# Message passing on a graph, edges sorted on the core: sums of the sort on ScalarE, portions cut anew

## The chip, the cores and the metric

One core of a Trainium2 chip runs the kernel. Its engines are named as in the profile: PE (TensorE, matrix products), DVE (VectorE), ACT (ScalarE), POOL (GpSimd) and SP (SyncE, which here only issues DMAs). Each has one queue that is worked off in order; an instruction that waits holds up all behind it. The metric is the device time of one execution in microseconds. The kernel before takes 10198.05 us, the median of three runs from 10188.47 to 10201.76.

## What is computed

12500 nodes with 64 features, 800000 edges with 4 features each, and a two-layer network on each edge whose results are added up at the edge's target node:

```python
def reference(x, e_attr, src, dst, w1, b1, w2, b2):
    N, D = x.shape
    h_src = x[src]
    h_dst = x[dst]
    m_in = jnp.concatenate([h_src, h_dst, e_attr], axis=-1)
    h = _silu(m_in @ w1 + b1)
    msg = h @ w2 + b2
    return _segment_sum(msg, dst, N)
```

N = 12500, D = 64, H = 128, E = 800000; `src` and `dst` are drawn at random and come in no order.

## The kernel before

**Algebra.** The first layer is split: `x @ w1[:64]` is a table in HBM (`Atab`, one row of 128 floats per node, gathered by `src`), `x @ w1[64:128] + b1` is a table in SBUF (`Btab`, for the targets), and the edge's own features are multiplied on the fly. The second layer comes after the sum over edges, so that the loop over edges only adds up `silu(...)` and a count in `S`.

**Sorting.** The targets are cut into R = 98 buckets of 128 nodes. For the loop over edges each batch of 512 slots must hold edges of few buckets. So the kernel sorts the edges itself, in portions: the edges stand as 6250 columns of 128, a group is PT = 40 columns, and `_PORTIONS` says how many groups each portion has. For a portion, `rank` works out each edge's slot within its group, then where the group's rows go; `place` builds the rows (16 records of 16 bf16 values, `CS` = 16) by products with one-hot matrices on PE and POOL scatters them into `buf` in HBM (two DMAs per half group, line 870).

**The batch loop** (`run`, line 1093 on) goes over 1590 batches of 512 slots. For batch n it loads records six and more batches ahead (`load`, by SP), makes indices (`sources`), gathers four times 128 rows of `Atab` on POOL (`gather`, line 1042, six batches ahead, `NGA` = 7 buffers), turns the records (`copies`, `turn`: ACT `rp`, PE, ACT `pts`), codes them (`code`: PE, ACT `oT`), adds the terms (`pre` on PE, `join` on DVE), applies `silu` on ACT, makes the segment matrix (`onehot`: PE, ACT `sg`), multiplies (`seg`, PE) and adds to `S` (`accum`, DVE). `turn`, `code`, `pre` and `onehot` share two PSUM buffers named `px`.

**How the two run together.** Portion 0 is sorted alone, at the start (`sort(ports[0])`), with one step of the generator `tables` after each `TEVERY`-th yield of the sort: 26 steps that multiply and store `Atab`, then 14 that scale `Btab` (ACT and POOL). Then `run` starts. `sure[k]` is the number of batches that are filled for certain when portions 0 to k are placed (`expected_batches`, from mean and spread of random buckets); phase k is the batches up to `sure[k]`. During phase k the function `filler` pulls steps out of two generators, `place` of portion k+1 and `rank` of portion k+2 (in phase 0 first `rank` of portion 1 alone), at rates in proportion to `place_cost` and `rank_cost`, so that they end twelve batches before the phase does. What is left then is run off with no batches beside it. In the last phase nothing is left to sort.

**Order.** Work that the sort gives to PE or ACT isn't put into the queue at once but at four fixed places of a batch: `later_pe` before `onehot` (place 2, first half of the batch) or at the batch's end (place 3); `later_act`, which the kernel before has but does not call, at the batch's end for the first half, and after `code` of the next batch (place 1) for the second. In the start, with no batches (`clock["now"]` is None), everything is issued at once.

**`rank` in ticks.** A portion is ranked in banks of QS = 5 columns, eight to a group. One pass of the loop `while done < ng` is a tick: it builds the one-hot matrices of one bank (`buckets`, line 420, DVE), then does one of three things: `counts` of a group, `bases` of a group, or `slots` of a bank. `slots` has PE add up in PSUM (`xp`, from two buffers named `rx`) each edge's rank for all 98 buckets, and two ticks later DVE multiplies each of the bank's five columns with its one-hot matrix and adds up along the row (line 525, with `accum_out`), which picks the edge's own slot. Each tick ends with `yield HALF`: this lane then has to wait for the next half of a batch, so at most two ticks fit in a batch. `yield HOP` has it wait for the next batch; the steps after the ticks (lines 580 to 727) have some ten.

Of the kernel before, what the change touches and what calls it, by code (L numbers as in the profile page):

```python
# [10 lines left out]
F32 = mybir.dt.float32  # L11
# [4 lines left out]
AF = mybir.ActivationFunctionType  # L16
OP = mybir.AluOpType
ET = mybir.EngineType

EP = 128  # L20
GT = 20
GE = EP * GT
PT = 2 * GT
# [9 lines left out]
HALF = -2.0  # L33
SUB = 5
QS = 5
NOH = 13
NGA = 7
TEVERY = 8
TAIL = 32
FR = 256 // CS  # L40
BIG = 262144.0
# [34 lines left out]
def tile_mpnn(ctx, tc, x, e_attr, src, dst, w1, b1, w2, b2, out, portions):  # L76
    nc = tc.nc
# [5 lines left out]
    R = (N + 127) // 128  # L83
    NP = R * 128
    VE, SC, GP, PE = nc.vector, nc.scalar, nc.gpsimd, nc.tensor

    last = len(portions) - 1
# [81 lines left out]
    for i in range(2):  # L169
        VE.tensor_scalar(t40[:, i * GT:(i + 1) * GT], iop[:, 0:1].to_broadcast([128, GT]), 2.0 * PT + i, None,  # L170
                         op0=OP.is_equal)
# [62 lines left out]
    wk = ctx.enter_context(tc.tile_pool(name="wk", bufs=2))  # L234
# [130 lines left out]
    def later_pe(f):  # L365
        later(f, 0, 2 + clock["half"])
# [8 lines left out]
    def rank(p):  # L375
        k, ng, cols = p["k"], p["ng"], p["cols"]
# [4 lines left out]
        slT = wk.tile([128, CM], F32, name="slT")  # L381
# [13 lines left out]
        def codes(c0):  # L395

            cn = min(4 * PT, cols - c0)
            raw = raws.pop(c0)
            VE.tensor_copy(d16[:EP, c0:c0 + cn], raw[:EP, :cn, 0])
            hl = wk.tile([128, 4 * PT], U16, name="hl", bufs=1)  # L400
            VE.tensor_scalar(hl[:EP, :cn], d16[:EP, c0:c0 + cn], 7, None, op0=OP.logical_shift_right)
            bk = wk.tile([128, 4 * PT], BF, name="bk")
            VE.tensor_copy(bk[:EP, :cn], hl[:EP, :cn])
            bks[c0 // (4 * PT)] = bk
            fetch(c0 + 8 * PT)

        ohs, bT, soon = {}, {}, {}
        tick = dict(t=0, cost=0.0, out=0)
        ready = {}

        def dve(d, f, cost, end=False):

            soon.setdefault((tick["t"] + d, end), []).append((f, cost))

        def buckets(g, c):

            n = min(QS, gts[g] - c * QS)
            oh = wk.tile([128, QS, R], BF, name="ohb", bufs=NOH)
            s0 = g % 4 * PT + c * QS
            VE.tensor_tensor(oh[:EP, :n], iob[:EP].unsqueeze(1).to_broadcast([EP, n, R]),  # L420
                             bks[g // 4][:EP, s0:s0 + n].unsqueeze(2).to_broadcast([EP, n, R]), op=OP.is_equal)
            ohs[g, c] = oh
# [53 lines left out]
        def bases(g):  # L476


            box = {}

            def f():
                bp = ps.tile([128, 512], F32, name="rx", bufs=2)
                PE.matmul(bp[:NR, :R], exz[:R], idf[:R, :R], start=True, stop=False)
                PE.matmul(bp[:NR, :R], fz[:R], trw[:R, :R], start=False, stop=True)
                box["bp"] = bp
            later_pe(f)

            def d0():
                bi = wk.tile([128, 128], I32, name="bi", bufs=1)
                VE.tensor_copy(bi[:NR, :R], box["bp"][:NR, :R])  # L490
                box["bi"] = bi

            def d1():
                bi = box["bi"]
                VE.tensor_tensor(bi[:NR, :R], bi[:NR, :R], bits[:NR].to_broadcast([NR, R]), op=OP.bitwise_and)

            def d2():
                b = wk.tile([128, 128], BF, name="bT")
                VE.tensor_copy(b[:NR, :R], box["bi"][:NR, :R])
                bT[g] = b  # L500
            dve(2, d0, 200.0)
            dve(2, d1, 200.0, True)
            dve(3, d2, 150.0)

        def slots(g, c):

            box = {}
            n = min(QS, gts[g] - c * QS)

            def f():  # L510
                xp = ps.tile([128, 512], F32, name="rx", bufs=2)
                oh = ohs[g, c]
                PE.matmul(xp[:EP, :n * R], triB[:EP, :EP], oh[:EP, :n].rearrange("p s b -> p (s b)"),
                          start=True, stop=False)
                for i in range(n):
                    s_ = c * QS + i
                    PE.matmul(xp[:EP, i * R:(i + 1) * R], selB[:NR, s_:s_ + 1].to_broadcast([NR, EP]),  # L517
                              bT[g][:NR, :R], start=False, stop=i == n - 1)
                box["xp"] = xp
            later_pe(f)  # L520

            def one(i):
                s_ = g * PT + c * QS + i
                oh = ohs[g, c]
                VE.scalar_tensor_tensor(oh[:EP, i], box["xp"][:EP, i * R:(i + 1) * R], 0.0, oh[:EP, i],  # L525
                                        op0=OP.add, op1=OP.mult, accum_out=slT[:EP, s_:s_ + 1])

            def last():
                ohs.pop((g, c))
                tick["out"] -= 1  # L530
            for i in range(n):
                dve(2, lambda i=i: one(i), 171.0)
            dve(2, last, 0.0)

        fetch(0)
        fetch(4 * PT)
# [4 lines left out]
        while done < ng:  # L541
            t = tick["t"]
            for f, c in soon.pop((t, False), []):
                f()
                yield c
            if coded * 4 < ng and nq > (ends[4 * coded - 5] if coded > 1 else -1):
                codes(coded * 4 * PT)
                coded += 1
                yield 450
            if nq < len(banks) and tick["out"] < NOH - 1:  # L550
                buckets(*banks[nq])
                if nq in ends:
                    ready["q", banks[nq][0]] = t
                nq += 1
                tick["out"] += 1
                yield 580.0
            for f, c in soon.pop((t, True), []):
                f()
                yield c
            if counted < ng and ready.get(("q", counted), t + 1) <= t:  # L560
                counts(counted)
                ready["c", counted] = t + 3
                counted += 1
            elif based < counted and ready["c", based] <= t:
                bases(based)
                ready["b", based] = t + 3
                based += 1
            elif nx < len(banks) and ready.get(("b", banks[nx][0]), t + 1) <= t:
                slots(*banks[nx])
                if nx in ends:  # L570
                    ready["s", banks[nx][0]] = t + 2
                nx += 1
            while done < ng and ready.get(("s", done), t + 1) <= t:
                done += 1
            tick["t"] += 1
            next(zeros, None)
            yield HALF
        for _ in zeros:
            pass
        for t in sorted(soon):  # L580
# [2 lines left out]
        ng = -(-cols // GT)  # L583
# [344 lines left out]
    def sort(p):  # L928
        yield from rank(p)
        yield from place(p)  # L930

    def rank_cost(p):
        return p["ng"] * (PT / QS * (880 + 580) + 2300 + 450 / 4 + 1300) + 10000

    def place_cost(p):
        return p["ng"] * (2000 + 2300 + 460 + PT / SUB * 1900)
# [24 lines left out]
    for i in range(NPT):  # L961
        t = cst.tile([65, 512], BF, name=f"pts{i}")
# [3 lines left out]
    for i in range(3):  # L966
        t = cst.tile([128, 4, H + 1], F32, name=f"h{i}")
# [96 lines left out]
    sums = {}  # L1064
# [84 lines left out]
    for i, _ in enumerate(sort(ports[0])):  # L1149
        if i % TEVERY == 0:  # L1150
            next(tg, None)
# [21 lines left out]
    def filler(m, part):  # L1173
        if part == 0:
            k = phase[m]
            if m == 0 or phase[m - 1] != k:
                if work["lanes"]:
                    settle()
                    while work["lanes"]:
                        for lane in work["lanes"]:  # L1180
                            for _ in lane["gen"]:
                                pass
                        work["lanes"] = []
                        if work["todo"]:
                            begin(m)
                    clock["now"] = m - LL
                work["until"] = sure[k] - LL - 2
                jobs = []
                if k + 1 < len(ports):
                    p = ports[k + 1]  # L1190
                    if k == 0:
                        work["todo"].append([(rank_cost(p), lambda p=p: rank(p))])
                    jobs.append((place_cost(p), lambda p=p: place(p)))
                if k + 2 < len(ports):
                    p = ports[k + 2]
                    jobs.append((rank_cost(p), lambda p=p: rank(p)))
                if jobs:
                    work["todo"].append(jobs)
                    begin(m - LL)
            return  # L1200
# [45 lines left out]
    for b0 in range(0, R, 4):  # L1246
# [6 lines left out]
        op = ps.tile([128, 512], F32, name="so", bufs=2)  # L1253
# [3 lines left out]
        for i in range(bn):  # L1257
            VE.scalar_tensor_tensor(ot[:, i], b2c, S[:, b0 + i, H:H + 1], op[:, i * D:(i + 1) * D],  # L1258
                                    op0=OP.mult, op1=OP.add)
# [6 lines left out]

_INS = ['x', 'e_attr', 'src', 'dst', 'w1', 'b1', 'w2', 'b2']
_OUTS = [((12500, 64), 'float32')]
_PORTIONS = [12, 8, 7, 9, 9, 12, 13, 11, 12, 13, 13, 13, 13, 12]


# [23 lines left out]
```

## Time and profile before

| | |
|---|---|
| median of three runs | 10198.05 us |
| profiled execution | 10154.93 us |
| its span, first to last instruction | 10153.1 us |
| mean granted clock of PE | 0.897 of full |
| instructions | 256393 |
| DMA | 563.40 MB, mean 55 GB/s |

How to read it: "busy" is the time in which an engine works on instructions, "idle before" is its idle time just before the instructions of a group, with what ended it. Register, branch and semaphore instructions and the issuing of DMAs are not busy time. A window's row gives for each engine the busy time and in brackets the number of instructions, then PE's granted clock, the share of the DMA engines and GB/s. Releasers are inferred. The durations of POOL's instructions are rough.

In forty equal slices of the span, a digit being tenths of the slice, the engines go like this:

```profile
PE   7788898999898998888998988989988988887774
DVE  6977887988798887777988888878878875542221
ACT  2044354444444444544444444444444444445552
POOL 3477577777777777777777777777777777777772
PEclk7888898999999999998999998999999999887776
```

### The profile page before, as it was taken

The numbers are of one execution on the slowest core, as the hardware profiler recorded it, in microseconds if no ns is written. First come the engines' busy times: TensorE is split into PE (matmuls) and PEld (weight loads), VectorE is DVE, ScalarE is ACT, GpSimd is POOL, SyncE is SP. The second block draws the span as 40 slices with busy tenths as digits, with TensorE's granted clock in tenths as the row PEclk, the third lists the DMA queues.
The fourth block names the chain that finished last, engine by engine and source line by source line (L and its number), as shares of the span: only waits on it lengthen the run. The fifth ranks groups of instructions, "written<-read, shape, count | busy, mean of one in ns | idle before, by whom it ended". The sixth has DMA issues, their size and how long they took to land. (4 is left out here: it accounts for less than half of the span.)

```text
span 10153.1 us, 256393 instructions
## 1 busy us (share of the span) xinstructions
PE 8728.9 (86%) x83393; PEld 7245.2 (71%) x83574; DVE 7601.7 (75%) x34618; ACT 4492.5 (44%) x8743; POOL 7351.0 (72%) x7072
## 2 busy tenths in 40 slices
PE   7788898999898998888998988989988988887774
PEld 5566776777777777776777777777777776666663
DVE  6977887988798887777988888878878875542221
ACT  2044354444444444544444444444444444445552
POOL 3477577777777777777777777777777777777772
PEclk7888898999999999998999998999999999887776
DMA  2022222222222222222222223222222222222332
GB/s 56 8 56 61 49 53 64 47 65 53 67 48 49 66 53 69 55 54 70 51 52 69 54 51 70 54 57 66 55 52 68 54 52 58 55 53 57 57 57 36
DMA packets 1176600, 563.40 MB, mean 55 GB/s; under 512 B 990738, under 2 KB 1066061, under 8 KB 1175136
## 3 DMA queue, kind: packets, MB, share of 16 engines
q0 software_dynamic: 223584, 443.00, 17.6%
q1 hardware_dynamic: 948234, 99.40, 6.8%
q8 instruction: 752, 12.32, 0.5%
q14 instruction: 712, 5.83, 0.2%
q10 hardware_dynamic: 3318, 2.85, 0.1%
HBM read 471.78 MB, written 88.20 MB: 55 GB/s over the span
## 5 line engine op out<-in xcount | busy, mean ns | idle before, releaser
L1042 POOL DMA_INDIRECT ga<-Atab,ix x6360 | 6475.6, 1018 | 2109.0 <-issue 1532.5
L1024 ACT ACTIVATE oT<-px,inv 128x512 bf16<-128x512 f32 x1590 | 1092.9, 687 | 3355.2 <-PE px L1022 3343.6
L1075 PE MATMUL so<-h,sg 128*128 128x129 f32 x12720 | 2405.6, 316 | 135.8 <-DVE S L1082 111.4
L909 PE MATMUL pl<-mk,oh 128*128 128x256 bf16 x18750 | 2364.2, 282 | 41.0 <-DVE oh L861 21.8
L909 PEld LDWEIGHTS <-oh 128*128 128x128 bf16 x18750 | 1861.2, 101 | 383.6 <-DVE oh L861 50.7
L1075 PEld LDWEIGHTS so<-h,sg 128*128 128x128 f32 x12720 | 1837.7, 208 | 321.3 <-DVE S L1082 165.3
L861 DVE TENSOR_SCALAR oh<-io,lo 128x384 bf16<-128x384 bf16 x6250 | 1811.9, 325 | 0.0
L1082 DVE TENSOR_TENSOR S<-S,so 128x129 f32 x3180 | 902.0, 284 | 1089.8 <-PE so L1075 1020.5
L1049 DVE TENSOR_TENSOR ga<-px,ga 128x512 f32<-128x512 f32 x1590 | 1089.7, 685 | 756.0 <-DMA ga<-Atab,ix 446.0
L1035 PE MATMUL px<-Btab,oT 128*128 x12720 | 1608.5, 236 | 3.2
L1033 PE MATMUL px<-WE,pts 65*128 65x128 bf16 x6360 | 1387.7, 238 | 17.1 <-DVE ga L1049 15.7
L1018 ACT ACTIVATE pts<-px 64x512 bf16<-64x512 f32 x1590 | 932.9, 587 | 809.7 <-PE px L1016 787.8
L1058 ACT ACTIVATE sg<-px 128x512 f32<-128x512 f32 x1590 | 947.1, 596 | 771.9 <-PE px L1056 748.2
L525 DVE SCALAR_TENSOR_TENSOR ohb<-rx,ohb 128x98 bf16<-128x98 f32 x6250 | 1271.6, 251 | 16.3 <-PE rx L517 15.8
L1056 PE MATMUL px<-CT,pts 65*128 65x128 bf16 x6360 | 636.9, 224 | 720.3 <-DVE ga L1049 375.7
L1056 PEld LDWEIGHTS <-pts 65*128 65x128 bf16 x6360 | 490.3, 100 | 1055.8 <-issue 1013.5
L1035 PEld LDWEIGHTS <-oT 128*128 128x128 bf16 x12720 | 1157.5, 108 | 89.5 <-issue 22.3
L854 DVE TENSOR_TENSOR mk<-q,pay 128x640 int32<-128x640 int32 x1250 | 1026.2, 821 | 179.8 <-PE pl L909 176.0
L870 POOL DMA_INDIRECT buf<-cb,idx x626 | 777.8, 1243 | 363.0 <-ACT carry L883 148.0
L1062 ACT ACTIVATE h<-ga 128x512 f32<-128x512 f32 x1590 | 985.5, 620 | 0.0
L420 DVE TENSOR_TENSOR ohb<-iob,bk 128x490 bf16<-128x490 bf16 x1250 | 834.8, 668 | 0.1
L1016 PE MATMUL px<-idb,rp 128*64 128x128 bf16 x6360 | 695.2, 236 | 57.7 <-DVE ga L1049 27.9
(313 smaller groups left out, 9076.2 us busy)
## 6 DMA issues: line engine op xcount, KB each, us to landing
ga<-Atab,ix POOLq DMA_INDIRECT x6360
buf<-zero SPq DMA_DIRECT2D x257, 128.0 KB
pld<-buf SPq DMA_DIRECT2D x1590, 16.0 KB
el<-in_e_attr_dram SPq DMA_DIRECT2D x73, 160.0 KB
buf<-cb,idx POOLq DMA_INDIRECT x626
Atab<-ga SPq DMA_DIRECT2D x24, 256.0 KB
sr<-in_src_dram SPq DMA_DIRECT2D x73, 80.0 KB
raw<-in_dst_dram SPq DMA_DIRECT2D x35, 160.0 KB
```

The lines of the kernel that those rows point to most:

```text
L525: VE.scalar_tensor_tensor(oh[:EP, i], box["xp"][:EP, i * R:(i + 1) * R], 0.0, oh[:EP, i], op0=OP.add, op1=OP.mult, accum_out=slT[:EP, s_:s ...
L854: VE.tensor_tensor(mk[:EP, :sn], q[:EP, s0:s0 + sn].unsqueeze(3).to_broadcast([EP, sn, CS, 8]), pay[:EP, go + s0:go + s0 + sn].bitcast(I32 ...
L861: VE.tensor_scalar(oh[:EP, i], io3[:EP], lo[:EP, go + s0 + i:go + s0 + i + 1], None, op0=OP.is_equal)
L909: PE.matmul(pa[:, u, :] if u < 2 else pb[:, :CS * PC], oh_[:, u * 128:(u + 1) * 128], mv, **fl)
L1024: SC.activation(oT, oq, AF.Relu, scale=inv[:, 0:1])
L1033: PE.matmul(pr[:, sl], pts[n % NPT][:, sl], WE, start=True, stop=False)
L1035: PE.matmul(pr[:, sl], s["oT"][:, sl], Btab[:, ds(v[t // 2], 1), u, :], start=False, stop=u == 1)
L1042: GP.indirect_dma_start(out=ga[:, t, :], out_offset=None, in_=Atab, in_offset=bass.IndirectOffsetOnAxis(ap=s["ix"][:, t:t + 1], axis=0))
L1049: VE.tensor_tensor(g, s["pr"], g, op=OP.add)
L1056: PE.matmul(sq[:, sl], pts[n % NPT][:, sl], CT, start=True, stop=True)
L1062: SC.activation(hs[n % 3][:, :, :H], st[n]["ga"], AF.Silu)
L1075: PE.matmul(so[u], s["sg"][:, t * 128:(t + 1) * 128], hs[n % 3][:, t, :], start=t == 2 * u, stop=t > 2 * u)
```

## The change

Five edits.

1. The sums over a bank's columns move. DVE makes one product over the whole bank of five columns (490 elements a partition) from `xp` in PSUM and the one-hot matrices into a new float tile `pr` with four buffers; ACT then adds up each of its five rows of 98 with a Copy that has `accum_out`, in place, put into ACT's queue by `later_act`. The one-hot buffers and the PSUM tile are given back after the product. In `rank` a bank is one entry on the list of DVE work (cost 580) instead of six (five of 171 and one of 0), so one yield instead of six.
2. For the portions before `FAST` = 6, `yield HALF` comes only after each second tick, otherwise `yield 0.0`: up to four ticks fit in a batch.
3. `TEVERY` is 16 instead of 8: a step of `tables` after each sixteenth yield of the sort of portion 0.
4. `_PORTIONS` has 16 entries instead of 14, the first with 10 groups instead of 12; `rank_cost` counts 580 + 580 per bank instead of 880 + 580.
5. `dynamic_dma_scratch_size` is 4096 instead of 8192.

```diff
-TEVERY = 8
+FAST = 6
+TEVERY = 16
...
-            def one(i):
-                s_ = g * PT + c * QS + i
-                oh = ohs[g, c]
-                VE.scalar_tensor_tensor(oh[:EP, i], box["xp"][:EP, i * R:(i + 1) * R], 0.0, oh[:EP, i],
-                                        op0=OP.add, op1=OP.mult, accum_out=slT[:EP, s_:s_ + 1])
-
-            def last():
-                ohs.pop((g, c))
+            def d():
+                pr = wk.tile([128, QS * R], F32, name="pr", bufs=4)
+                VE.tensor_tensor(pr[:EP, :n * R], box["xp"][:EP, :n * R],
+                                 ohs.pop((g, c))[:EP, :n].rearrange("p s b -> p (s b)"), op=OP.mult)
                 tick["out"] -= 1
-            for i in range(n):
-                dve(2, lambda i=i: one(i), 171.0)
-            dve(2, last, 0.0)
+
+                def sums():
+                    for i in range(n):
+                        s_, row = g * PT + c * QS + i, pr[:EP, i * R:(i + 1) * R]
+                        SC.activation(row, row, AF.Copy, accum_out=slT[:EP, s_:s_ + 1])
+                later_act(sums)
+            dve(2, d, 580.0)
...
-            yield HALF
+            yield HALF if k >= FAST or tick["t"] % 2 == 0 else 0.0
...
-        return p["ng"] * (PT / QS * (880 + 580) + 2300 + 450 / 4 + 1300) + 10000
+        return p["ng"] * (PT / QS * (580 + 580) + 2300 + 450 / 4 + 1300) + 10000
...
-_PORTIONS = [12, 8, 7, 9, 9, 12, 13, 11, 12, 13, 13, 13, 13, 12]
+_PORTIONS = [10, 5, 7, 5, 8, 8, 12, 12, 12, 12, 12, 12, 10, 10, 11, 11]
...
-    nc = _bacc.Bacc("TRN2", target_bir_lowering=False, num_devices=1, dynamic_dma_scratch_size=8192)
+    nc = _bacc.Bacc("TRN2", target_bir_lowering=False, num_devices=1, dynamic_dma_scratch_size=4096)
```

## Prediction

> **What bounds the kernel now.** The page first: no engine of it is full by its busy share.
>
> ```profile
> span 10153.1 us, 256393 instructions
> PE 8728.9 (86%) x83393; PEld 7245.2 (71%) x83574; DVE 7601.7 (75%) x34618; ACT 4492.5 (44%) x8743; POOL 7351.0 (72%) x7072
> L1042 POOL DMA_INDIRECT ga<-Atab,ix x6360 | 6475.6, 1018 | 2109.0 <-issue 1532.5
> L870 POOL DMA_INDIRECT buf<-cb,idx x626 | 777.8, 1243 | 363.0 <-ACT carry L883 148.0
> ```
>
> POOL's 72% misleads, which its timeline shows, in the middle of the run and in the tail:
>
> ```profile
> 7102.80 0.94 POOL L1042 DMA_INDIRECT ga<-Atab,ix  x1 [0.30 <-issue]
> 7104.04 0.94 POOL L1042 DMA_INDIRECT ga<-Atab,ix  x1 [0.30 <-issue]
> 7105.29 1.01 POOL L870 DMA_INDIRECT buf<-cb,idx  x1 [0.30 <-issue]
> ...
> 9500.08 0.94 POOL L1042 DMA_INDIRECT ga<-Atab,ix  x1 [0.30 <-ACT pts L1018]
> ...
> 9511.30 0.94 POOL L1042 DMA_INDIRECT ga<-Atab,ix  x1 [0.30 <-issue]
> ```
>
> Every instruction follows the last by the same 0.30 us, whoever is named. The nine steps from 9500.08 to 9511.30 take 11.22 us, 1.247 each: a gather costs 0.94 plus a fixed 0.305. So I count POOL as occupied in these gaps. Next the table by stage, with borders where the first gather of each portion's first batch is issued:
>
> ```profile
> core 0: us, PE busy (x) PEld busy (x) DVE busy (x) ACT busy (x) POOL busy (x), PEclk, DMA share, GB/s
> 0.00:323.00 323.00, 243.89 (x1507) 176.95 (x1507) 231.98 (x1461) 61.61 (x141) 96.55 (x85) 0.73 0.16 45
> 323.00:565.00 242.00, 189.11 (x1539) 147.66 (x1537) 220.17 (x756) 21.34 (x49) 155.71 (x49) 0.95 0.04 11
> 565.00:1214.00 649.00, 560.70 (x5269) 458.60 (x5271) 518.30 (x2648) 262.42 (x497) 437.08 (x421) 0.83 0.25 58
> 1703.00:2124.00 421.00, 381.49 (x3839) 318.45 (x3841) 386.53 (x1856) 172.18 (x335) 297.28 (x276) 0.94 0.23 53
> 6119.00:6863.00 744.00, 675.48 (x6738) 566.13 (x6753) 618.39 (x2843) 351.12 (x684) 570.63 (x558) 0.93 0.26 59
> 9135.00:9975.00 840.00, 649.66 (x4920) 524.17 (x4920) 233.85 (x685) 440.99 (x836) 635.05 (x672) 0.75 0.31 57
> 9975.00:10153.00 178.00, 56.47 (x359) 52.65 (x358) 24.60 (x110) 18.45 (x32) 0.00 (x0) 0.60 0.15 29
> ```
>
> Three parts: a start of 565 us without gathers (portion 0 is ranked until 312, its scatter rows are worked out until 323, it is placed until 565), 9410 us of batches, an end of 178. In the batches POOL issues 6360 gathers and 578 scatters (48 of the 626, 155.5 us of them, stand in the start). Busy 6475.6 + 622.3 = 7098, gaps 6938 x 0.305 = 2116, together 9214: 196 us are left in which POOL truly idles, 2% of this part. They lie early. In 565:1214, 649 - 437 - 421 x 0.305 leaves 84; in 1703:2124 it leaves 40; in 6119:6863 3. **POOL bounds the batches; DVE and PE bound the start and a few short portions.** What DVE saves elsewhere shortens nothing.
>
> From the same table, per batch: with no sorting beside it (168 batches in 9135:9975) POOL 5.00 us, DVE 1.39, PE 3.87 at clock 0.75, or 2.9 at full. In 1703:2124 60 batches stand beside 360 columns ranked and 360 placed, 6 per batch: POOL needs (297.3 + 276 x 0.305)/60 = 6.36, so 0.227 us more per column, which is its two scatters per 20 columns and gathers drawn out. In 6119:6863 (126 batches, 520 columns) DVE spends (618 - 126 x 1.39)/520 = 0.85 us a column.
>
> **The change, part by part.** The sums on DVE, as the timeline has them:
>
> ```profile
> 270.38 0.66 DVE L420 TENSOR_TENSOR ohb<-iob,bk 128x490 bf16<-128x490 bf16 x1
> 270.96 0.25 DVE L525 SCALAR_TENSOR_TENSOR ohb<-rx,ohb 128x98 bf16<-128x98 f32 x1
> 271.14 0.08 DVE L525 DVE_READ_ACCUMULATOR ohb<-rx,ohb 128x1 f32 x1
> 271.14 0.25 DVE L525 SCALAR_TENSOR_TENSOR ohb<-rx,ohb 128x98 bf16<-128x98 f32 x1
> ...
> L1049 DVE TENSOR_TENSOR ga<-px,ga 128x512 f32<-128x512 f32 x1590 | 1089.7, 685 | 756.0 <-DMA ga<-Atab,ix 446.0
> ```
>
> A sum is listed with 0.25 us, but the next starts after 0.18, so a bank of five costs 0.90. The product that replaces them has PSUM and SBUF sources as L1049 has: 685 ns for 512 elements, some 0.66 for 490, and 0.60 to the next start (L420's 0.66 leaves 0.58). DVE saves **0.30 us a bank**, 375 us over 1250 banks, 0.06 a column (0.79 left).
>
> ACT gets 6250 small sums. No row has one. From
>
> ```profile
> L1062 ACT ACTIVATE h<-ga 128x512 f32<-128x512 f32 x1590 | 985.5, 620 | 0.0
> L1009 ACT ACTIVATE rp<-pld 128x256 bf16<-128x256 bf16 x1590 | 655.7, 412 | 5.5 <-DMA pld<-buf 5.5
> ...
> 103.21 0.38 ACT L291 ACTIVATE ga<-so 128x256 f32<-128x256 f32 x1 [4.41 <-PE so L288]
> 103.49 0.38 ACT L292 ACTIVATE S<-so 128x256 f32<-128x256 f32 x1
> ```
>
> 256 elements more cost 208 ns, so 98 take 0.28 us, and 0.18 between starts (0.10 overlaps, as in the last two rows). Reading out the sum costs nothing at best, a whole further instruction (the 0.20 of a line through zero elements) at worst: 0.18 to 0.49 each. I take 0.26, near DVE's own read-out of 0.08. That is 1625 us more on ACT, 44% to 60%, hidden as long as ACT stays ahead of PE and POOL. Behind a burst of five in ACT's queue stand `sg` of the same batch, or `rp` and `pts` of the next, on which PE waits for its PSUM buffers.
>
> The Trainium skill (ScalarE: Activation LUTs, Rules for kernel authors) speaks against this edit: adds and multiplies belong on VectorE, which is faster per element. By engine time alone it is right here, 375 saved against 1625 spent, and the sum would be a loss; the occupied gaps of POOL say that neither engine is the bound, so I don't follow it.
>
> *Start.* Rank of portion 0:
>
> ```profile
> 19.00:170.00 151.00, 31.51 (x300) 0.94 0.28 76
> 170.00:246.00 76.00, 35.62 (x316) 0.50 0.00 1
> 246.00:300.00 54.00, 28.61 (x261) 0.50 0.01 1
> L293 DVE TENSOR_REDUCE top<-so 128x1 f32<-128x256 f32 (+1 forms) x50 | 20.9, 419 | 52.8 <-ACT S L292 52.6
> ```
>
> (The first three are windows of L525 alone; its counts hold a read-out beside each sum.) Undisturbed, after 246, 130 sums in 54 us: a group of 40 columns takes 16.6 us. Twelve would take 199, not 293: some 80 us are the 26 steps of the tables up to 170 (3.1 each, mostly DVE waiting in order for PE and ACT), some 14 the later steps, in which POOL works on `Btab`. After: ten groups at 16.6 - 8 x 0.30 = 14.2, say 14.5, make 145. A bank now gives three yields instead of eight, so rank of ten groups has about 310; a table step every 16 reaches 20 of the 26 steps there, 62 us. Ten groups are placed in 10/12 of 242, 202, plus 18 for the other six steps and 20 for `Btab` beside the scatters. 19 + 145 + 62 + 12 + 202 + 38 = **478, 87 less**. If ACT needs 0.49 a sum, 40 of them are 19.6 us a group and rank takes some 36 more; if the spread tables hide fully, some 90 less.
>
> *Early portions.* The kernel's own rule for batches that are surely complete gives 97, 84, 60, 99, 90 batches to the first portions before, and 80, 55, 58, 51, 88, 64, 133 after. Rank takes some 13 ticks and 10 for each group (one for each of its eight banks' slots, one for its counts, one for its bases, never two in one tick), until now two per batch: portions 1 and 2 needed 88 batches and some 20 for their last steps (about ten hops each, of a batch or more), while portion 0 gave 85 (97 less the lead of 12); the rest ran with no batches beside it, which I read as the 84 us. With four ticks per batch 146 ticks need 37 + 20 of 68. I leave 30 us there. Two phases grow dense: 51 batches beside 320 + 320 columns (6.27 a batch) and 64 beside 480 + 480 (7.5). DVE needs 1.39 + 0.79 x 6.27 = 6.35 us and 7.3; at the 0.92 that it reached in 1703:2124, 6.9 and 7.95, against POOL's 6.42 and 6.70: 25 and 80 us idle. Portion 7 is beyond FAST, and its 133 ticks need 67 + 10 batches of 62: 20 more. Idle in all 155 for 196, **41 less**; bounds 95 (no dense loss at half) and 280.
>
> *Nothing.* 1590 batches still hold all rows, so the gathers stay. Gathers are drawn out by other DVE work as well; rank's share is bounded by the means with place alone and with both:
>
> ```profile
> L1042 POOL DMA_INDIRECT ga<-Atab,ix x517 | 512.2, 991 | 157.5 <-issue 125.8 <-DMA ga<-Atab,ix 4.9 <-ACT h L1062 4.3
> L1042 POOL DMA_INDIRECT ga<-Atab,ix x517 | 531.8, 1029 | 157.6 <-issue 125.2 <-DMA ga<-Atab,ix 4.0 <-DVE oh L861 4.0
> ```
>
> (8405:9135, then 7644:8405.) 0.038 us, some 200 over 5200 gathers, shared with L420, which stays: I take 0, bounds -60 and +60. With 40 scatters in the start instead of 48, eight more cost 1.38 each, **11 more**. The clearing DMAs on SP, a few per cent more rows, the two extra portion ends and the smaller DMA scratch I take at 0, under POOL's queue.
>
> Sum: -87 - 41 + 11 = -117. The profiled execution took 10154.93 us, 2 around its span and 43 below the median 10198; I take the difference off the median: **10080 us**.
>
> **Rivals.**
> *ACT reaches PE* (slower). In 6119:6863 PE idles 744 - 675 = 69 us, 0.55 per batch; POOL stays fed while ACT's delay to PE is below that. A batch has 0.83 banks, 1.08 us of sums (2.0 at 0.49). It decides where more than half arrives. At three quarters, 0.81 - 0.55 = 0.26 for some 1100 batches with rank beside them: 10080 + 286 = 10370. For it: PE is 91% busy, in order, with two PSUM buffers for all steps of a batch. Against: ACT is 47% busy there.
> *The dense phases eat the gain.* DVE at 0.85 instead of 0.92 idles POOL 54 and 122 us, portion 7's overrun 60, the start saves only 55: -55 + 70 + 11, 10224.
> *More gain.* Tables hide (-90), idle 95 (-60): 9930.
> *The scratch.* If with half the descriptor space each of 6938 DMA instructions waits a tenth of its gap longer, 0.03 us, 208 more eat the gain: 10290. Against it: the constant gap above shows no waiting at the present size.
>
> **How the numbers follow.** Forecast 0.52 (own range 9970 to 10190: start bounds and gathers), more gain 0.13, dense phases 0.10, ACT 0.20, scratch 0.05. A measurement of this kernel tells about 0.2%, 20 us. Faster: 0.50 + 0.13 = 0.63; within: 0.02 + half of the dense phases = 0.07; slower 0.30. The range 9950 to 10340 leaves out half of "more gain" and somewhat over half of ACT.
>
> **What would show it.** First gather near 478 (430 to 520). Sums on ACT near 0.26 between starts. POOL's gaps at 0.30 in the middle, gather mean near 1.02; true idle near 155, in the phases from batches 193 and 332. DVE's busy time lower by some 375. Wrong: POOL idle spread over all batches with PE waiting for `sg`, `pts` or `oT`, gaps above 0.30, or a start past 520.

## The result, and the profile after

The changed kernel takes 10290.99 us, median of five runs (10254.16 to 10295.15), against 10188.47 us for the kernel before in the same session: **1.0093 times as long, interval 1.0072 to 1.0114**. Forecast was 10080, 1% faster. It is slower, by about as much.

The page of the changed kernel, busy times first, then the groups of its gathers and of the new sums and product:

```profile
span 10287.8 us, 257725 instructions
PE 8885.8 (86%) x83728; PEld 7342.1 (71%) x83728; DVE 7301.7 (71%) x23457; ACT 6041.1 (59%) x21243; POOL 7374.5 (72%) x7072
...
L1043 POOL DMA_INDIRECT ga<-Atab,ix x6360 | 6512.5, 1024 | 2222.1 <-issue 1467.7
...
L532 ACT ACTIVATE pr<-pr 128x98 f32<-128x98 f32 x6250 | 1677.6, 275 | 38.1 <-DVE pr L525 34.6
...
L532 ACT ACTIVATION_READ_ACCUMULATOR pr<-pr 128x1 f32 x6250 | 1202.0, 192 | 0.0
...
L525 DVE TENSOR_TENSOR pr<-rx,ohb 128x490 f32<-128x490 f32 x1250 | 822.9, 659 | 91.6 <-PE rx L518 69.1
```

DVE is busy 300 us less (375 were forecast) and ACT 1549 us more, as the change means it to be. Where the time went is seen only by stages; the borders are again the first gathers of phases (columns: window, its length, busy us and instructions of PE, its weight loads, DVE, ACT and POOL, clock, DMA share, GB/s):

```profile
0.00:515.00 515.00, 379.12 (x2587) 286.01 (x2587) 382.28 (x1155) 186.05 (x983) 223.34 (x126) 0.75 0.11 31
515.00:1033.00 518.00, 442.58 (x4120) 361.73 (x4121) 372.80 (x1225) 333.65 (x1365) 348.01 (x340) 0.82 0.24 59
...
1374.00:1746.00 372.00, 326.89 (x3185) 269.65 (x3184) 284.56 (x922) 238.89 (x948) 260.21 (x252) 0.89 0.23 56
1746.00:2122.00 376.00, 329.96 (x3346) 274.87 (x3345) 324.11 (x1062) 230.20 (x932) 250.79 (x238) 0.95 0.21 51
2122.00:2672.00 550.00, 492.03 (x4831) 409.06 (x4828) 425.03 (x1372) 362.10 (x1429) 394.73 (x384) 0.89 0.23 57
2672.00:3208.00 536.00, 485.14 (x4691) 399.81 (x4692) 467.72 (x1522) 311.41 (x1329) 336.78 (x305) 0.90 0.19 47
3208.00:9307.00 6099.00, 5460.27 (x53020) 4544.97 (x53020) 4526.47 (x14543) 3746.21 (x12751) 4704.71 (x4555) 0.92 0.24 58
...
10093.00:10288.00 195.00, 53.20 (x340) 48.89 (x337) 24.04 (x108) 17.31 (x30) 0.28 (x1) 0.58 0.14 27
```

Read POOL with its gap of 0.305 us per instruction. In the long window, batches 396 to 1433, it leaves 6099 - 4705 - 4555 x 0.305 = 5 us: POOL bounds the middle as before. In the windows ahead of it 66, 35, 53, 38 and 106 us are left (phases 0, 2, 3, 4 and 5); phase 1, which is not shown, leaves 4. The whole account, profile against profile:

| term | before | after | change | forecast |
|---|---|---|---|---|
| start, until the first gather | 565 | 515 | -50 | -87 |
| idle time of POOL beyond its gaps (the expectations below say 196 and 312, from slightly other borders) | 195 | 309 | +114 | -41 |
| gathers, busy | 6476 | 6512 | +36 | 0 |
| scatters among the batches, with gaps | | | +18 | +11 |
| end, after the last gather | 179 | 195 | +16 | 0 |
| sum | | | +134 | -117 |

### The profile page after: what moved, and what is told of

It is laid out like the page before. It is cut to its first block, busy times and chain, and to the rows that moved or that the text cites. A ratio compares the mean times of both kernels' runs of the same rounds, so it can differ in the third digit from the quotient of the medians.

```text
span 10287.8 us, 257725 instructions
## 1 busy us (share of the span) xinstructions
PE 8885.8 (86%) x83728; PEld 7342.1 (71%) x83728; DVE 7301.7 (71%) x23457; ACT 6041.1 (59%) x21243; POOL 7374.5 (72%) x7072
## 5 line engine op out<-in xcount | busy, mean ns | idle before, releaser
L910 PE MATMUL pl<-mk,oh 128*128 128x256 bf16 x18750 | 2392.9, 283 | 42.1 <-DVE oh L862 31.4
L862 DVE TENSOR_SCALAR oh<-io,lo 128x384 bf16<-128x384 bf16 x6250 | 1851.0, 331 | 0.1
L532 ACT ACTIVATE pr<-pr 128x98 f32<-128x98 f32 x6250 | 1677.6, 275 | 38.1 <-DVE pr L525 34.6
L1036 PE MATMUL px<-Btab,oT 128*128 x12720 | 1690.0, 235 | 4.3
L1034 PE MATMUL px<-WE,pts 65*128 65x128 bf16 x6360 | 1416.4, 238 | 98.0 <-ACT sg L1059 93.4
L532 ACT ACTIVATION_READ_ACCUMULATOR pr<-pr 128x1 f32 x6250 | 1202.0, 192 | 0.0
L871 POOL DMA_INDIRECT buf<-cb,idx x626 | 725.6, 1159 | 250.2 <-issue 137.4
L525 DVE TENSOR_TENSOR pr<-rx,ohb 128x490 f32<-128x490 f32 x1250 | 822.9, 659 | 91.6 <-PE rx L518 69.1
```

What stands on the lines that cost most here:

```text
L532: SC.activation(row, row, AF.Copy, accum_out=slT[:EP, s_:s_ + 1])
L862: VE.tensor_scalar(oh[:EP, i], io3[:EP], lo[:EP, go + s0 + i:go + s0 + i + 1], None, op0=OP.is_equal)
L910: PE.matmul(pa[:, u, :] if u < 2 else pb[:, :CS * PC], oh_[:, u * 128:(u + 1) * 128], mv, **fl)
L1034: PE.matmul(pr[:, sl], pts[n % NPT][:, sl], WE, start=True, stop=False)
L1036: PE.matmul(pr[:, sl], s["oT"][:, sl], Btab[:, ds(v[t // 2], 1), u, :], start=False, stop=u == 1)
```

## The experiments

All ratios are to the kernel before, on the same chip and with their 95% interval. "Start", "idle" and "end" are taken from each run's profile in the same way as above. Two such profiles of kernels that differ in nothing that matters show idle 195 and 219 (the kernel before, and the run with its scratch alone), so some 25 us of idle is the noise of one profile. Four kernels with the same start as the kernel before, itself among them, begin their batches between 560 and 577, so a start is good to some 15 us. The kernels with sums on ACT and fourteen or fifteen portions have three `pr` buffers, not four.

**The sums back on DVE, the rest as changed.**

```diff
-                VE.tensor_tensor(pr[:EP, :n * R], box["xp"][:EP, :n * R],
...
-                later_act(sums)
+                VE.scalar_tensor_tensor(oh[:EP, i], box["xp"][:EP, i * R:(i + 1) * R], 0.0, oh[:EP, i],
+                                        op0=OP.add, op1=OP.mult, accum_out=slT[:EP, s_:s_ + 1])
```

> The changed kernel with its sums taken back to DVE (five fused products with sum per bank, cost 880 again); portions, FAST, TEVERY and scratch stay as changed. The changed kernel stands at 1.009 of the kernel before, and POOL idles 312 us beyond its gaps in the batches, against 196 before, nearly all of it in the phases up to batch 396. Theory A, the short and dense first portions starve POOL and ACT has no part in it: idle here is as large or larger (310 to 400 us, since DVE has 0.06 us a column more), the ratio to the kernel before 1.010 to 1.020. Theory B, bursts of sums in ACT's queue hold up PE's buffers: idle falls to 200 or less and the ratio is below 1.002.

Measured: 1.0004 (0.9996 to 1.0013), start 485, idle 266, gathers 6476, end 195. Neither theory is right alone: the ratio is B's, but 266 us of idle remain with no sum on ACT, so most of the idle time is of the portions and ticks. Read the other way round, the same pair says what the sums on ACT cost beside the other four edits: 0.9%.

**The sums on ACT in the kernel before.**

```diff
+                VE.tensor_tensor(pr[:EP, :n * R], box["xp"][:EP, :n * R],
...
+                later_act(sums)
...
-dynamic_dma_scratch_size=8192
+dynamic_dma_scratch_size=4096
```

> The kernel before with edit 1 alone: one product on DVE and five sums on ACT per bank, cost 580; old portions, no FAST, TEVERY 8. Scratch 4096, and pr with three buffers instead of four, for SBUF space. Theory A: DVE's saving shortens the start by some 20 to 40 us and the idle time of 196 us a little; ratio 0.990 to 0.997. Theory B: POOL idles 260 us or more although the portions are old, and the ratio is above 1.003.

Measured: **0.9950 (0.9937 to 0.9963)**, start 535, idle 129, gathers 6532. The ratio and the start are theory A's, the idle time falls more than it said. By itself, the edit that the change is named for is a gain: 30 us of start and 66 of idle, less 56 us by which the gathers get longer.

**The old portions in the changed kernel.**

```diff
-_PORTIONS = [10, 5, 7, 5, 8, 8, 12, 12, 12, 12, 12, 12, 10, 10, 11, 11]
+_PORTIONS = [12, 8, 7, 9, 9, 12, 13, 11, 12, 13, 13, 13, 13, 12]
```

> The changed kernel with the fourteen old portions, all else as changed (pr with three buffers for SBUF space). Theory A: start near 560 (twelve groups), idle below 150 us since no phase is shorter than before and ticks come faster; ratio 0.985 to 0.995. Theory B: idle 250 us or more, ratio 1.00 to 1.01.

Measured: 1.0049 (1.0036 to 1.0062), start 581, idle 200. A's numbers fail: with the old portions the kernel is still slower. It differs from the one just shown in FAST and TEVERY only, and those two cost a whole percent. Neither theory had named them.

**No FAST in the changed kernel.**

```diff
-FAST = 6
+FAST = 0
```

> The changed kernel with FAST = 0, so never more than two ticks in a batch. If the lumps of up to two ticks in one half of a batch are what holds up PE and ACT (theory C), idle in phases 0 to 4 falls from 200 us to below 100 and the ratio is below 1.005. If the ticks are needed (theory A, and my prediction's reading), the ranks of the first portions no longer end in time, whole stretches of sorting run with no batches beside them, idle grows beyond 400 us and the ratio is above 1.02.

Measured: 1.0055 (1.0042 to 1.0068), idle 227 (124 in phases 0 to 4, against 197). The direction is theory C's, the size falls short: the idle time of these phases falls by 73 us, where 100 or more were expected, and the ratio stays above 1.005. That the ranks need four ticks a batch, as my prediction read it, is refuted: without them the kernel is faster.

**TEVERY 8 in the changed kernel.**

```diff
-TEVERY = 16
+TEVERY = 8
```

> The changed kernel with a table step after each 8th yield again (TEVERY 8). The kernel with the old portions and TEVERY 16 starts its batches at 581 us, the one with TEVERY 8 at 535. Theory D, a table step costs more beside place than beside rank, so spreading the tables lengthens the start: start 515 falls to 465 to 480, batches unchanged, ratio to the kernel before 1.004 to 1.006. My prediction's reading, that the steps cost 3 us wherever they stand and place hides the later ones: start stays at 505 to 520, ratio 1.008 to 1.010.

Measured: 1.0052 (1.0033 to 1.0070), start 472, batches as long as before the edit (9569 us for 9579). Theory D holds. The two stages of the start, rank and then place, in the changed kernel

```profile
20.00:265.00 245.00, 216.22 (x1367) 163.77 (x1368) 165.28 (x524) 155.01 (x926) 12.32 (x25) 0.62 0.16 44
265.00:515.00 250.00, 161.64 (x1219) 121.63 (x1217) 206.19 (x565) 31.04 (x57) 203.66 (x76) 0.85 0.03 9
```

and with TEVERY 8:

```profile
20.00:281.00 261.00, 211.39 (x1373) 159.96 (x1374) 196.53 (x533) 168.76 (x943) 89.90 (x60) 0.69 0.16 42
281.00:472.00 191.00, 149.78 (x1213) 117.57 (x1211) 165.82 (x554) 17.23 (x40) 145.35 (x41) 0.95 0.04 12
```

With TEVERY 8 all 40 table steps fall into rank, with 16 only 25; the fifteen that move shorten rank by 16 us and lengthen place by 59. POOL's 35 instructions more in the second stage (76 for 41) are those on `Btab` and the clearing of `S`. DVE's busy time there grows by 40 us with hardly an instruction more (565 for 554). Most of it is the one-hot matrices of place, in the changed kernel and then with TEVERY 8:

```profile
L862 DVE TENSOR_SCALAR oh<-io,lo 128x384 bf16<-128x384 bf16 x370 | 127.9, 401 | 0.0
```

```profile
L862 DVE TENSOR_SCALAR oh<-io,lo 128x384 bf16<-128x384 bf16 x370 | 93.7, 308 | 0.0
```

In the changed kernel their mean is 533 ns until 397 us, while POOL works on `Btab` and `S`, and 338 after it. The rest of the 59 us is a wait, because the scatters stand behind that work in POOL's queue (instructions of POOL, ACT and DVE, in order of time):

```profile
313.44 47.64 POOL L309 TENSOR_TENSOR Btab<-S,Btab 128x896 f16<-128x896 f32 x2
...
376.59 1.05 POOL L871 DMA_INDIRECT buf<-cb,idx  x1 [0.17 <-issue]
...
380.13 0.60 ACT L887 ACTIVATE cb<-pl 128x512 bf16<-128x512 f32 x1 [32.10 <-DMA buf<-cb,idx]
...
384.61 2.69 DVE L855 TENSOR_TENSOR mk<-q,pay 128x640 int32<-128x640 int32 x1 [25.22 <-PE pl L910]
```

Two such products take 3.6 us at other times and 47.64 here; ACT waits 32.10 us for a scatter to land before it may write `cb` again, PE waits for ACT, and DVE idles 25.22 us. Why POOL's product takes so long there was not tried by itself.

**Sums on ACT and FAST, old portions, TEVERY 8.** Against the kernel with the sums on ACT shown above:

```diff
+FAST = 6
...
-            yield HALF
+            yield HALF if k >= FAST or tick["t"] % 2 == 0 else 0.0
```

> The kernel before with sums on ACT and FAST = 6, TEVERY 8, old portions. Without FAST this kernel stands at 0.995 with 129 us idle; with FAST and TEVERY 16 at 1.005 with 200. Theory C, up to four ticks in a batch bunch the ranks and idle POOL: idle 180 to 220 and start 535, ratio 0.999 to 1.002. Rival, FAST is harmless and TEVERY 16 alone made the difference: idle 120 to 140, ratio 0.994 to 0.996.

Measured: 1.0000 (0.9990 to 1.0010), start 540, idle 208. Theory C, to the number: FAST takes back the whole 0.5% that the sums had gained. Both kernels rank portion 1 in the same 80 us of phase 0. Without FAST:

```profile
565.00:645.00 80.00, 73.16 (x778) 60.12 (x778) 54.92 (x155) 72.82 (x325) 60.79 (x64) 0.93 0.27 57
```

With FAST:

```profile
565.00:645.00 80.00, 65.61 (x610) 52.18 (x610) 55.62 (x142) 66.15 (x358) 40.22 (x42) 0.71 0.16 38
```

64 instructions of POOL become 42, sixteen batches ten and a half, and PE, DVE and ACT all have room: over the 80 us nobody is full, each waits for another. The waits of this window with FAST name the ring (who waits, for whom, us in total, times, longest):

```profile
POOL ga L1043 <- ACT h L1063: 15.3, 5, 5.8
DVE pr L525 <- ACT pr L532: 13.7, 12, 3.9
...
POOL ga L1043 <- DVE bi L491: 9.9, 2, 9.6
...
PE rx L514 <- DVE pr L525: 5.2, 6, 1.1
...
PE rx L432 <- DVE pr L525: 4.8, 3, 2.4
```

POOL idles 27 us here beyond its gaps. The 15.3 for `silu` are the ring's; one wait of 9.6 us for DVE need not be, since the kernel with FAST and the sums on DVE has one of 8.0 in the same stage. Two or three banks a batch put ten or fifteen sums into ACT's queue at two places of a batch. DVE's next product waits until ACT has given back one of the `pr` buffers, PE waits for the PSUM buffer that this product reads, `silu` stands behind all of it, and POOL waits for the gather buffer that `silu` reads. PE's granted clock, 0.93 without FAST, is 0.71 with it. The changed kernel in the same stage:

```profile
560.94 0.27 ACT L532 ACTIVATE pr<-pr 128x98 f32<-128x98 f32 x1
561.11 0.19 ACT L532 ACTIVATION_READ_ACCUMULATOR pr<-pr 128x1 f32 x1
561.20 0.58 ACT L1059 ACTIVATE sg<-px 128x512 f32<-128x512 f32 x1
561.68 0.27 ACT L532 ACTIVATE pr<-pr 128x98 f32<-128x98 f32 x1
...
564.35 0.40 ACT L1010 ACTIVATE rp<-pld 128x256 bf16<-128x256 bf16 x1
...
565.65 0.68 ACT L1025 ACTIVATE oT<-px,inv 128x512 bf16<-128x512 f32 x1
566.22 0.28 ACT L532 ACTIVATE pr<-pr 128x98 f32<-128x98 f32 x1
```

Ten sums stand between `sg` and `rp` (561.68 to 564.35, 0.267 each), five more ahead of the next `sg`: 15 x 0.267 + 2.4 for the batch's own five = 6.4 us a batch on ACT, more than POOL's 5.0 (80 us for 64 instructions, four a batch, in the window without FAST). So in its fullest batches ACT alone needs more than POOL.

**FAST alone, sums on DVE.** The same edit in the kernel before.

> The kernel before with FAST = 6 alone, sums on DVE. If bunched ranks idle POOL by themselves (theory C as it stands): idle 240 to 290 us against 195, ratio 1.004 to 1.008. If they do so only through bursts of ten sums in ACT's queue (theory B and C together): idle 130 to 195, since no sorting is left over at the ends of phases, ratio 0.994 to 1.000.

Measured: 1.0006 (0.9993 to 1.0018), start 566, idle 234. In between the two theories: without sums on ACT, FAST costs nothing that can be measured, and gains nothing either. POOL's waits for a gather buffer in the kernel before (in all, times, longest):

```profile
POOL ga L1042 <- ACT h L1062: 207.0, 183, 36.1
```

And with FAST:

```profile
POOL ga L1043 <- ACT h L1063: 225.1, 193, 6.9
```

The longest wait, 36.1 us of sorting left over at the end of phase 0, is gone, as FAST means it to be; the sum of the waits is no smaller: in the first 240 us of phase 0 POOL idles 32 us with FAST and none without.

**The scratch alone.**

```diff
-dynamic_dma_scratch_size=8192
+dynamic_dma_scratch_size=4096
```

> The kernel before with the DMA scratch of 4096 alone. My prediction takes 0: ratio 0.999 to 1.001, gather mean 1.018 us, gaps 0.305. Rival, the smaller scratch draws out POOL's DMA instructions, and with it the 55 us that the gathers take longer in all kernels with sums on ACT (all of which have 4096): gather mean 1.025 or more, ratio 1.004 to 1.007.

Measured: 1.0003 (0.9992 to 1.0013). The row of its gathers among the batches:

```profile
L1042 POOL DMA_INDIRECT ga<-Atab,ix x6360 | 6465.9, 1017 | 2134.3 <-issue 1475.1 <-ACT h L1062 236.2 <-DMA ga<-Atab,ix 135.6
```

1017 ns for 1018: the smaller scratch costs nothing here and is not what makes the gathers longer.

**Sums on ACT and the new portions, without FAST, TEVERY 8.**

```diff
-FAST = 6
-TEVERY = 16
+FAST = 0
+TEVERY = 8
```

> The changed kernel without FAST and with TEVERY 8, so sums on ACT, the sixteen new portions and the smaller scratch. It closes the account: from the sums alone (start 535, idle 129, end 180) the new portions should take some 64 us off the start (472 as with TEVERY 8 before), add 80 to 110 us of idle (most of it in phase 5, where 64 batches stand beside 480 + 480 columns), 15 at the end (26 instead of 22 tests of the batch count) and 18 of scatters: ratio 0.998 to 1.003. Rival, the new portions are only bad together with FAST: idle 150 or less, ratio 0.992 to 0.996.

Measured: 1.0001 (0.9991 to 1.0011), start 463, idle 231 (92 of it in phase 5), end 195. The account closes: the new portions take 73 us off the start and put 102 of idle and 15 of end in their place; the gathers are 22 us shorter than with the sums alone, the scatters take 6 more.

**One test of the batch count instead of 22, in the kernel before.**

```diff
-TAIL = 32
+TAIL = 800
```

> The kernel before with TAIL 800 instead of 32: the batches beyond 1590, which this input doesn't fill, are tested for once instead of 22 times. In the traces each test takes PE about 5 us at the end (112 us for 22, 132 for 26). If so, the end falls from 179 to 70 to 80 us and the ratio is 0.989 to 0.991. Rival, the tests run beside the last batches' work: no change.

Measured: 0.9887 (0.9870 to 0.9904), end 69. PE's first product after the batches, in the kernel before, the changed one and this one:

```profile
L1250 PE MATMUL px<-idf,S 128*128 128x128 f32 x98 | 18.2, 328 | 113.3 <-PEq L1242 111.8 <-ACT ga L1252 1.5
```

```profile
L1251 PE MATMUL px<-idf,S 128*128 128x128 f32 x98 | 17.5, 318 | 134.3 <-PEq L1243 132.6 <-ACT ga L1253 1.7
```

```profile
L1250 PE MATMUL px<-idf,S 128*128 128x128 f32 x98 | 17.7, 322 | 5.4 <-DVEq L1242 3.8 <-ACT ga L1252 1.6
```

111.8 us for 22 tests is 5.1 each; 26 tests, since sixteen portions reserve 2392 batches at most where fourteen reserve 2289, take 132.6. They skip code that never runs here. The idle time of this profile, 211, is that of the kernel before within the noise: the gain is in the end, as expected, 109 us of it.

**Both gains together, and with portions that grow evenly.** The first has the sums on ACT and TAIL 800, the second besides:

```diff
-_PORTIONS = [12, 8, 7, 9, 9, 12, 13, 11, 12, 13, 13, 13, 13, 12]
+_PORTIONS = [10, 7, 7, 8, 9, 10, 11, 11, 12, 12, 12, 12, 12, 12, 12]
```

> Sums on ACT in the kernel before (old portions, no FAST, TEVERY 8) together with TAIL 800. The two gains add up if they are independent: 0.995 and 0.990 give 0.983 to 0.987.

> The same with fifteen portions that grow evenly: 10, 7, 7, 8, 9, 10, 11, 11, then seven of 12; no phase has over 6 columns sorted per batch. Theory: start 472 instead of 535, idle 130 to 200 (the ranks of portions 1 and 2 still don't end in phase 0), 0.977 to 0.984. Rival, a shorter first portion gives back in idle all that the start gains: 0.984 to 0.988.

Measured: 0.9838 (0.9824 to 0.9851), which is the product of the two gains, and **0.9810 (0.9797 to 0.9824), 9982.20 us**, which beats both kernels. The second starts at 468 instead of 540 and idles 195 us instead of 149: here a short first portion gives back less than it gains. That this is because no later phase is dense was the theory and fits (163 of the 195 us lie in phases 0 to 2), but was not tried by itself. Start, idle and ratio of the second are inside the theory's ranges.

## Why the prediction was wrong

**The step that failed** is "Idle in all 155 for 196, 41 less". Measured were 309, and these 154 us are the largest part of the 251 between the forecast change, -117, and the measured one, +134. The prediction costed each phase by its mean, so many columns over so many batches, with DVE as the engine that could fall behind, and took from FAST only that the ranks would end in time. Phase 5, where the density is real and no rank is fast, came out as forecast (100 for 106: one wait of 37 us for the ranks left over, forecast 20, and 69 spread over the phase, forecast 80). Phases 0, 2, 3 and 4 were put at 55 and took 66 + 35 + 53 + 38 = 192.

FAST did what it was meant to do, and it was no gain. The kernel with sums on ACT and old portions, with and without it, shows this best. Counted by DVE's products between two `silu`, it ranks portion 1, 64 banks, with three banks in most batches under FAST: 15 of the 64 before the first `silu` and 49 in the 17 batches behind it. Without FAST it is 2 and then 62 in 41 batches, mostly one or two each. In the first 240 us of phase 0 POOL idles 65 us with FAST and none without; behind them it idles 26 instead of 67, since one wait of 36 us for sorting left over at the phase's end is gone. Together that is 91 for 67. POOL runs at most six batches ahead, so what it loses in the crowded batches isn't made up for: where it idles nothing anyway, fewer ranks beside a batch win nothing. With the sums on DVE the same 240 us idle 32 under FAST, and again none without: the sums on ACT double what the crowded batches cost. This is the rival of ACT reaching PE, but in another place: I had it in all batches with rank beside them, and it shows only up to batch 396.

Of the 197 us in phases 0 to 4 of the changed kernel, 73 go without FAST; with the old portions and the sums on ACT it is 208 against 129 in all. In phases 2 and 3 the banks come only a little denser than without FAST (1.6 and 1.8 a batch while a portion is ranked, against 1.5); that FAST idles POOL there through the same ring is not shown. What makes the other 124 stays open. Phase 4, in which no rank is fast, idles 24 to 38 us in the four kernels with sums on ACT and the new portions, and 3 in the one with sums on DVE, which speaks for ACT's sums; but that one idles 76 us in phase 3 instead of 53 to 55, so that with FAST the two phases together idle 79 us there and 79 to 91 here.

**The start** was put at 478 and came out at 515, by two sizes of its sum. Rank and its last steps were to end at 238 and ended at 265: 25 table steps fell into it, not 20, some 16 us at 3.1 each, and 11 more are open. Place was to take 202 and 38 for what is left of the tables, and took 250: with no table step in it, with TEVERY 8, it takes 191, so the fifteen steps cost 59, twenty of them having been put at 38. With TEVERY 8 the start is 463 to 472. Edit 1 is part of this: with the sums on DVE a bank gives eight yields, so that even with TEVERY 16 all table steps fall into rank, and the start is 485.

**Taken at nothing.** The gathers: 36 us longer, inside the bounds of 60. The two further portion ends: 16 us at the end, from the tests, which I had not looked at, though PE's 112 us of waiting for its own queue stood in a row of the profile of before. The scratch: nothing, rightly.

**Right.** POOL bounds the batches (5 us left of 6099); the price of a sum on ACT (0.26 taken, 0.267 measured) and that ACT's 1549 us more hide in the long run; and that edit 1 need not be a loss for taking more of ACT than it saves of DVE. The rule that adds and multiplies belong on VectorE (the Trainium skill, ScalarE: Activation LUTs, Rules for kernel authors) would have had the sums alone as a loss; they measure 0.995. Beside the other four edits the sums are a loss, of 0.9%. Edit by edit: the sums 0.9950, with the new portions 1.0001, with FAST 1.0052, with TEVERY 16 1.0093. In this order one edit gains, three cost 0.4 to 0.5% each, and the scratch does nothing. The order matters: without the sums on ACT, FAST costs nothing (1.0006), and the new portions, FAST and TEVERY 16 together cost nothing either (1.0004). What is lost is lost by the sums on ACT and these edits together.

## What to carry to other kernels

When a queue with a short lead bounds a pipeline, price a schedule by its fullest stretch, not by the mean of a phase: work that is moved forward is not made up for by the empty stretch behind it. Measure a bundle of edits one by one, both on the version without the others and on the version with them: here the same edit gained 0.5% alone and cost 0.9% in company. Look at the end of the profile as well: tests for work that never comes were the dearest thing that could be taken out (1.1%).

## What the hardware showed besides

A ScalarE sum over 98 elements has two rows, 0.275 us and a read-out of 0.192, and 0.267 us between starts, 0.09 more than the 0.18 worked out for a plain one. A test whose block is skipped, on all engines, took 5.1 us here (111.8 for 22), and the single one left 3.8. Beside POOL's work on `Btab`, DVE's one-hot matrices took 533 ns each instead of 338, and one pair of POOL's products 47.64 us. POOL's gathers take 6492 to 6533 us in all in the nine kernels with sums on ACT and 6466 to 6476 in the five with sums on DVE; the scratch isn't the cause, and what is stays open.
